# Sigmoid attention with a gated dense stage: the first group's keys cast and turned tile by tile, its values loaded as fp32 by SyncE

## The chip, the cores and the metric

The kernel runs on one core of a Trainium2 chip. The metric is the device time of one execution in microseconds (us); the time before is the median of 3 runs. Engines are named as in the profile: PE (TensorE, matmuls; PEld its weight loads), DVE (VectorE), ACT (ScalarE), POOL (GpSimd), SP (SyncE).

## The reference

```python
# q, k, v: (8, 12, 448, 64) fp32
scores = np.matmul(q, k.transpose(0, 1, 3, 2)) / np.sqrt(64) - np.log(448)
attn = 1.0 / (1.0 + np.exp(-scores))               # a sigmoid for each score, no sum over keys
x = np.matmul(attn, v)                             # (8, 12, 448, 64)
x = x.transpose(0, 2, 1, 3).reshape(8 * 448, 768)  # a token's 12 heads side by side
h = x @ w_in                                       # w_in (768, 2048)
g = h * (1.0 / (1.0 + np.exp(-beta * h)))
out = g @ w_out                                    # w_out (2048, 768), out (3584, 768) fp32
```

## The kernel before

Everything is computed in fp16 with fp32 sums. The 12 heads of a batch element are 3 groups of 4 heads (group g: batch element g // 3); a group's q and k are 128 rows of 32 positions times 4 heads, each row holding 14 blocks of 64 numbers. In such a row, position and head dimension are exchanged by a transpose of 32 x 32 squares on DVE (`transpose`, L196 for queries, L204 and L208 for keys), which reads pairs of fp16 as one 32-bit word. Keys are used in 3 tiles of 128 (`jt` 0 to 2) and a last one of 64 (`jt` 3); the word order of the raw row interleaves the three tiles (blocks i, j with i = 0..3 outside and tile j = 0..2 inside), and L204 sorts them while it turns them.

For a tile of keys, PE computes scores (`score`, L218) into a score tile of two PSUM banks, ACT takes the sigmoid of it into fp16 (`weigh`, L230), and `attend` (L291) multiplies by the values into a PSUM tile that DVE casts into `xT` (L300). `dense1` multiplies `xT` by `w_in` (L171), ACT and DVE apply the gate (L317, L320), and the result lies in `gt`; `dense2` and later steps multiply by `w_out`.

The order is written out by hand under `manual_schedule`, each engine working through its own list. The change lies in the first 20 us, where batch element 0 is begun with the first half of its queries (224 positions):

- SP loads group 0's q (first half) and k as fp32 into `staged`, a piece of `gt` that is still unused; then beta (L756). DVE and ACT cast them into the fp16 tile `raws[0]` (L747, L749, L750): of the keys, ACT the second half of the columns and DVE the first. DVE turns the queries and then all the keys.
- POOL loads the rest with DMAs that cast on the way (`load_one` L115, `load_v` L136 and L143, `load_w_in` L153), in the order q, k of groups 1 and 2, values of batch element 0 for all 12 heads (six DMAs: four for the 3 full tiles, two for the last 64 keys), the queries' second halves, and the 8 chunks of `w_in`, each for two of the 16 column blocks `dc` of `dense1`. At most eight POOL DMAs are under way: each waits for the landing of the eighth before it.
- `half_visit(g, c0, second)` computes the scores of group g for a half of the queries: key tiles 0 and 1 first, then with `second` tiles 2 and 3, with two score tiles each time. In this stage three score tiles exist (`share_psum(..., 3, 2)`), and two further banks, which `bank` gives out by turns for idle units and for `attend`.
- Idle units (`idle_units`, L740) are matmuls on zeros whose result nobody reads, 10 and a short one at the start, 4 (at the end 2) between half visits.
- `double_v_last` (L146) copies the values of the last 64 keys into the other 64 partitions; odd slots read them there.

The middle of it reads:

```python
        for g in range(QPB):
            for second in range(2):
                half_visit(g, 0, second)
                if 2 * g + second < 2 * QPB - 1:
                    idle_units(4 if g < QPB - 1 else 2)
        double_v_last(0)
        transpose(0, 0, NH, NB)
        attend(0, 0, QH)
        half_visit(0, QH, 0)
        attend(1, 0, QH)
```

After `attend(2, ...)` the PSUM banks are dealt out anew and `dense1` of the first 16 column blocks begins, mixed with the other half visits; then follows the long list of `STEPS`.

Of the kernel before, what the change touches and what calls it, by code (L numbers as in the profile page):

```python
# [8 lines left out]
FP32 = mybir.dt.float32  # L9
FP16 = mybir.dt.float16  # L10
# [3 lines left out]
def kernel(  # L14
# [10 lines left out]
    nc = tc.nc  # L25
# [3 lines left out]
    B, H, S, D = q.shape  # L29
    NTOK, DM = out.shape  # L30
    DFF = moe_w_in.shape[1]
    P = 128
    BLK = 32
    HQ = P // BLK
    NB = S // BLK
    PAIR = D // BLK
    JF = S // P
    KL = S - JF * P
    NF = JF * P // BLK
    NPAIR = H // 2  # L40
    QPB = H // HQ
# [5 lines left out]
    QH = S // 2  # L47
# [7 lines left out]
    vp = ctx.enter_context(tc.tile_pool(name="vp", bufs=2))  # L55
    qTp = ctx.enter_context(tc.tile_pool(name="qTp", bufs=3))
    kTp = ctx.enter_context(tc.tile_pool(name="kTp", bufs=3))
# [27 lines left out]
    def touch(i: int):  # L85
        used[i] = max(used.values()) + 1


    def bank(name: str, cols: int = S, hold=None):
        i = min((i for i in used if i not in held.values()), key=used.get)  # L90
        touch(i)
        if hold is not None:
            held[hold] = i
        pool = psum["one" if i < N_ONE else "late"]
        return pool.tile([P, cols], FP32, tag=f"one{i}", name=name)
# [12 lines left out]
    raws = {}  # L108
    vs = {}
# [19 lines left out]
    def last_base(s: int) -> int:  # L129
        return (s % 2 ^ swapped(s // 2)) * KL  # L130

    def load_v(b: int):
        vs[b] = vp.tile([P, H, JF + 1, D], FP16, tag="v16", name="v16")
        rows = v[b].rearrange("h (p c) d -> p h (c d)", c=NB)
        for i in range(HQ):
            nc.gpsimd.dma_start(  # L136
                out=vs[b][i * BLK : (i + 1) * BLK, :, 0:JF].rearrange("p h j d -> p h (j d)"),
                in_=rows[:, :, JF * i * D : JF * (i + 1) * D],
            )
        rows = v[b].rearrange("h (p c) d -> p h c d", c=NB)  # L140
        for c in range(NF, NB):
            lo = (c - NF) * BLK
            nc.gpsimd.dma_start(out=vs[b][lo : lo + BLK, :, JF], in_=rows[:, :, c])  # L143

    def double_v_last(b: int):
        nc.vector.tensor_copy(out=vs[b][KL:P, :, JF], in_=vs[b][0:KL, :, JF])  # L146

    WCH = 8
    WOUT = 2
# [30 lines left out]
    kT = {}  # L180
# [10 lines left out]
    def transpose(g: int, r: int, c0: int = 0, c1: int = NB):  # L191
        raw = raws[g][:, r]
        if r == 0:
            if g not in qT:
                qT[g] = qTp.tile([P, NB * BLK, PAIR], FP16, tag="qT", name="qT")
            nc.vector.transpose(  # L196
                out=in_order(g // QPB, qT[g][:, c0 * BLK : c1 * BLK]),
                in_=raw[:, c0:c1].rearrange("p c d -> p (c d)").bitcast(FP32),
            )
            return  # L200
        kT[g] = kTp.tile([P, S, PAIR], FP16, tag="kT", name="kT")
        to = kT[g].rearrange("p k e -> p (k e)").bitcast(FP32)
        frm = raw.rearrange("p c d -> p (c d)").bitcast(FP32).rearrange("p (c f) -> p c f", c=NB)
        nc.vector.transpose(  # L204
            out=to[:, 0 : JF * P].rearrange("p (j i q) -> p i j q", j=JF, i=HQ),
            in_=frm[:, 0:NF].rearrange("p (i j) f -> p i j f", j=JF),
        )
        nc.vector.transpose(  # L208
            out=to[:, JF * P :], in_=frm[:, NF:].rearrange("p c f -> p (c f)")
        )  # L210
# [45 lines left out]
    def half_visit(g: int, c0: int, second: int):  # L256
        slots = (2 * g, 2 * g + 1)
        scos = [score_tile() for _ in slots]
        plan = [(s, jt, sco, jt * QH) for jt in (0, 1) for s, sco in zip(slots, scos)]
        widths = [S, S]  # L260
        if second:
            plan = [(s, 2, sco, 0) for s, sco in zip(slots, scos)]
            plan += [(s, JF, scos[0], QH) for s in slots]
            widths = [S, QH]
        for i in range(0, len(plan), 2):
            for e in range(PAIR):
                for s, jt, sco, u0 in plan[i : i + 2]:
                    for hh in range(2):
                        score(sco, u0, s, jt, hh, e, c0, QH)
        homes = [None, None]  # L270
        if c0 == 0 and g < QPB - 1:
            home = outp.tile([P, 2 * S], FP32, tag="osb", name="early")
            home = home.bitcast(FP16).rearrange("p (x h s) -> p x h s", x=2, h=2)
            homes = [home[:, x] for x in range(2)]
        ats = {id(sco): weigh(sco, n, at) for sco, n, at in zip(scos, widths, homes)}
        for s, jt, sco, u0 in plan:
            at_tiles[s, jt, c0] = ats[id(sco)][:, :, u0 : u0 + QH]
# [435 lines left out]
    with tc.manual_schedule():  # L713
        raws[0] = rawp.tile([P, 2, NB, D], FP16, tag="raw", name="raw")
        wide = gt.rearrange("p a b -> p (a b)").bitcast(FP32)
        cut = NH * D
        early = [(0, 0, NH), (1, 0, NB)]
        staged = {}
        at = 0
        for r, c0, c1 in early:  # L720
            staged[r] = wide[:, at : at + (c1 - c0) * D]
            at += (c1 - c0) * D
            nc.sync.dma_start(  # L723
                out=staged[r],
                in_=(q, k)[r][0, 0:HQ].rearrange("h (p c) d -> (h p) (c d)", c=NB)[
                    :, c0 * D : c1 * D
                ],
            )
        nc.gpsimd.memset(dummy, 0.0)
        nc.scalar.activation(out=dummy, in_=dummy, func=AF.Sigmoid, bias=0.0, scale=1.0)  # L730

        still = gt[:, NDC - 1, 0:512]
        nc.vector.memset(still, 0.0)
        beta_in = sigp.tile([P, S], FP32, tag="sg", name="beta_in")[0:BLK, 0:P]
        nc.vector.memset(beta_in, 0.0)
        idle = bank("idle_ps", 512)

        def idle_units(n: int, cols: int = 512):
            for _ in range(n):
                nc.tensor.matmul(  # L740
                    idle[:, 0:cols], still[:, 0:P], still[:, 0:cols], start=True, stop=True
                )

        idle_units(10)
        idle_units(1, 256)
        raw = raws[0].rearrange("p r c d -> p r (c d)")
        nc.vector.tensor_copy(out=raw[:, 0, 0:cut], in_=staged[0])  # L747
        transpose(0, 0, 0, NH)
        nc.scalar.copy(out=raw[:, 1, cut:], in_=staged[1][:, cut:])  # L749
        nc.vector.tensor_copy(out=raw[:, 1, 0:cut], in_=staged[1][:, 0:cut])  # L750
        transpose(0, 1)
        for g in range(1, QPB):
            load_one(g, 0, 0, NH)
            load_one(g, 1)
        load_v(0)
        nc.sync.dma_start(out=beta_in[0:NDC], in_=moe_beta.rearrange("(c p) -> c p", p=P))  # L756
        for g in range(QPB - 1):
            load_one(g, 0, NH, NB)
        for c in range(WCH):
            if c == WCH // 2:  # L760
                load_one(QPB - 1, 0, NH, NB)
            load_w_in(c)
        for g in range(1, QPB):
            transpose(g, 0, 0, NH)
            transpose(g, 1)

        for g in range(QPB):
            for second in range(2):
                half_visit(g, 0, second)
                if 2 * g + second < 2 * QPB - 1:  # L770
                    idle_units(4 if g < QPB - 1 else 2)
        double_v_last(0)
        transpose(0, 0, NH, NB)
        attend(0, 0, QH)
        half_visit(0, QH, 0)
        attend(1, 0, QH)
        half_visit(0, QH, 1)
        for g in range(1, QPB - 1):
            transpose(g, 0, NH, NB)
        attend(2, 0, QH, (0,))  # L780
        attend(2, 0, QH, (1,))
        for i in range(P // BLK):
            part = slice(i * BLK, (i + 1) * BLK)
            nc.vector.transpose(out=beta_sb[part], in_=beta_in[:, part])
        load_qk(QPB)
        load_qk(QPB + 1)
        load_v(1)
        load_w_out(0, 0)
        load_w_out(1, 0)
        load_qk(QPB + 2)  # L790
        load_w_out(0, 1)
        load_w_out(1, 1)

        firsts.close()
        share_psum(ctx, seconds, 2, N_ONE, 2)
        first_half(4)
        half_visit(1, QH, 0)
        first_half(3)
        half_visit(1, QH, 1)
        transpose(2, 0, NH, NB)  # L800
        attend(0, QH, QH)
        first_half(1)
        half_visit(2, QH, 0)
        first_half(4)
        half_visit(2, QH, 1)
        attend(1, QH, QH)
        first_half(3)
        attend(2, QH, QH)
        first_half(1)
        follow(STEPS)  # L810
# [30 lines left out]
```

## Time and profile before

| | |
|---|---|
| time, median of 3 runs | 368.29 us (367.94 to 368.37) |
| the profiled execution | 368.51 us, of which the span of its instructions is 366.7 us |
| PE busy | 361.6 us, 99% |
| DVE, ACT, POOL busy | 271.7, 248.7, 154.3 us |
| granted TensorE clock in the profile's row | 1.0 throughout |
| DMA engines, first eight slices (73 us) | busy share 8 or 9 tenths |

Times in the profile count from the first instruction of the span. A row of the timeline has the start, the length, the engine, the line, what is written from what with the shapes, the number of instructions merged into it, and in brackets how long the engine had been idle and what released it. The chain of waits follows the work that ended last back to the start; a row of it is start, length, what. A DMA's row has the issuing engine, the count, the size, and the time from issue to landing.

### The profile page before, as it was taken

How to read it: one execution, taken by the hardware profiler on the slowest of the kernel's cores; microseconds unless marked ns; L12 is line 12 of the kernel's file. 1: busy time of each engine (PE TensorE's matmuls, PEld its weight loads, DVE VectorE, ACT ScalarE, POOL GpSimd, SP SyncE). 2: the span in 40 equal slices, each digit the busy share in tenths (PEclk: the TensorE clock that was granted, in tenths of full speed). 3: DMA queues.
4: the chain of work that ended last, by engine and by line, in shares of the span. 5: the costliest groups of instructions: out<-in, count | busy, mean ns of one | idle time of the engine just before them, and what ended most of it. 6: DMA issues, size and time to landing. Idle time of an engine off the chain costs nothing.

```text
span 366.7 us, 9126 instructions
## 1 busy us (share of the span) xinstructions
PE 361.6 (99%) x3677; PEld 238.0 (65%) x3677; DVE 271.7 (74%) x521; ACT 248.7 (68%) x409; POOL 154.3 (42%) x192
## 2 busy tenths in 40 slices
PE   8999999999999999999999999999999999999996
PEld 3478754457465685557857667666856687679763
DVE  3356569889995796876778678868878667678764
ACT  4987976789765797657865579977874859226410
POOL 7834523504413873117761445841630316316610
PEclk9999999999999999999999999999999999999999
DMA  8999999930363790416919363373303030030234
GB/s 168 184 197 201 199 206 198 236 39 2 50 139 52 160 152 2 74 64 111 156 13 149 52 137 52 49 81 89 52 1 89 2 88 2 0 88 0 56 68 138
DMA packets 42698, 34.76 MB, mean 95 GB/s; under 512 B 21904, under 2 KB 39200, under 8 KB 42656
## 3 DMA queue, kind: packets, MB, share of 16 engines
q0 software_dynamic: 36688, 22.47, 44.8%
q1 hardware_dynamic: 5968, 11.71, 11.5%
q8 instruction: 29, 0.48, 0.6%
q14 instruction: 13, 0.11, 0.1%
HBM read 45.62 MB, written 11.01 MB: 154 GB/s over the span
## 4 chain that ended last, share of the span: by engine, by line
PE 93%; DMA 3%; ACT 2%; DVE 1%; SPq 0%; issue 0%; ACTq 0%; DVEq 0%
PE m_ps L171 71%; PE sco L218 12%; PE av_ps L291 9%; DMA out_dram<-osb 2%; ACT attnT L230 1%; PE idle_ps L740 1%; DMA gt<-in_k_dram 1%; DVE osb L372 0%; SPq L602 0%; ACT osb L425 0%; DVE xT L300 0%; DVE kT L204 0%; ACT raw L749 0%; ACT osb L463 0%; SPq L723 0%
## 5 line engine op out<-in xcount | busy, mean ns | idle before, releaser
L230 ACT ACTIVATE attnT<-sco 128x896 f16<-128x896 f32 (+1 forms) x163 | 139.2, 908 | 37.8 <-PE sco L218 37.1
L372 DVE TENSOR_TENSOR osb<-m_ps,osb 128x448 f32<-128x448 f32 (+2 forms) x197 | 116.3, 596 | 51.1 <-PE m_ps L171 42.0
L171 PEld LDWEIGHTS <-w_in 128*128 128x128 f16 (+1 forms) x948 | 81.0, 100 | 18.8 <-issue 11.0
L171 PE MATMUL m_ps<-xT,w_in 128*128 128x224 f16 (+3 forms) x750 | 85.5, 266 | 0.3 <-ACT attnT L230 0.2
L492 POOL TENSOR_TENSOR gt<-osb,sg 128x448 f16<-128x448 f32 x26 | 29.5, 1135 | 117.8 <-ACT sg L425 107.7
L502 POOL TENSOR_TENSOR gt<-osb,sg 128x448 f16<-128x448 f32 x52 | 58.3, 1138 | 35.1 <-ACT sg L425 33.5
L425 ACT ACTIVATE sg<-osb,beta_sb 128x224 f32<-128x224 f32 (+1 forms) x104 | 54.0, 575 | 10.3 <-DVE osb L372 10.0
L171 PEld LDWEIGHTS <-sum 128*128 128x128 f16 (+1 forms) x444 | 39.9, 99 | 27.4 <-issue 3.6
L171 PEld LDWEIGHTS <-gt 128*128 128x128 f16 (+1 forms) x474 | 36.9, 102 | 25.7 <-issue 7.5
L171 PE MATMUL m_ps<-w_out,gt 128*128 128x384 f16 (+2 forms) x350 | 52.6, 324 | 0.0
L218 PE MATMUL sco<-qT,kT 32*128 32x448 f16 (+3 forms) x864 | 51.5, 340 | 0.3 <-ACT attnT L230 0.2
L171 PEld LDWEIGHTS <-w_S 128*128 128x128 f16 (+1 forms) x486 | 43.9, 99 | 7.0 <-issue 6.0
L171 PE MATMUL m_ps<-w_out,sum 128*128 128x384 f16 (+1 forms) x228 | 40.6, 327 | 0.0
L171 PE MATMUL m_ps<-w_T,sum 128*128 128x384 f16 (+1 forms) x216 | 40.3, 326 | 0.0
L300 DVE CAST xT<-av_ps 128x448 f16<-128x448 f32 (+1 forms) x54 | 28.4, 566 | 14.2 <-PE av_ps L291 14.1
L291 PE MATMUL av_ps<-attnT,v 128*64 128x448 f16 (+3 forms) x400 | 38.2, 343 | 0.0
L171 PE MATMUL m_ps<-xs,w_S 128*128 128x224 f16 (+1 forms) x330 | 36.2, 259 | 0.0
L291 PEld LDWEIGHTS <-v 128*64 128x64 f16 (+1 forms) x432 | 20.4, 108 | 17.7 <-issue 9.8
L425 ACT ACTIVATE osb<-m_ps,beta_sb 128x224 f32<-128x224 f32 x52 | 20.4, 448 | 15.4 <-PE m_ps L171 15.1
L218 PEld LDWEIGHTS <-kT 32*128 32x128 f16 (+1 forms) x864 | 13.5, 96 | 23.1 <-issue 21.5
L320 DVE TENSOR_TENSOR gt<-m_ps,sg 128x224 f16<-128x224 f32 (+1 forms) x40 | 16.6, 434 | 12.5 <-ACT sg L317 12.2
L463 ACT COPY osb<-m_ps 128x448 f32<-128x448 f32 x26 | 13.8, 535 | 17.7 <-PE m_ps L171 15.5
(50 smaller groups left out, 303.5 us busy)
## 6 DMA issues: line engine op xcount, KB each, us to landing
out_dram<-osb SPq DMA_DIRECT2D x100, 96.0 KB, 2.4
raw<-in_k_dram POOLq DMA_DIRECT2D x23, 224.0 KB, 5.7
raw<-in_q_dram POOLq DMA_DIRECT2D x21, 224.0 KB, 4.4
v<-in_v_dram POOLq DMA_DIRECT2D x32, 144.0 KB, 7.0
w_in<-in_moe_w_in_dram POOLq DMA_DIRECT2D x8, 384.0 KB, 10.3
w_out<-in_moe_w_out_dram POOLq DMA_DIRECT2D x4, 768.0 KB, 13.1
v<-in_v_dram POOLq DMA_DIRECT2D x16, 48.0 KB, 6.4
out_dram<-osb SPq DMA_DIRECT2D x4, 192.0 KB, 2.4
```

Source lines behind the costliest of these rows:

```text
L171: nc.tensor.matmul(to[c : c + step], hidden[:, c : c + step], weights, **({} if step == P else {"tile_position": (0, c)}), **flags,)
L218: nc.tensor.matmul(sco[base : base + nk, hh, u0 : u0 + n], kT[g][lo : lo + BLK, jt * P : jt * P + nk, e], qT[g][lo : lo + BLK, c0 : c0 + n ...
L230: nc.scalar.activation(out=at[:, :, 0:n], in_=sco[:, :, 0:n], func=AF.Sigmoid, bias=NEG_LOG_S, scale=MSCALE,)
L291: nc.tensor.matmul(av[hh * D : (hh + 1) * D, 0:n], vs[b][base : base + nk, 2 * (s % NPAIR) + hh, jt], at[base : base + nk, hh, 0:n], start ...
L300: nc.vector.tensor_copy(out=xTs[b][:, s % NPAIR, c0 : c0 + n], in_=av[:, 0:n])
L320: nc.vector.tensor_tensor(out=gt[:, dc, off : off + n], in0=m1[:, 0:n], in1=sg[:, 0:n], op=ALU.mult)
L372: nc.vector.tensor_tensor(out=out, in0=in0, in1=in1, op=op)
L425: nc.scalar.activation(out=out, in_=in_, func=AF.Sigmoid, bias=0.0, scale=beta_sb[:, dc : dc + 1])
L463: nc.scalar.copy(out=oa[:, 0], in_=m)
L492: nc.gpsimd.tensor_tensor(out=gt[:, 2 * d : 2 * d + 2, off : off + QH], in0=ob[:, 0], in1=sg, op=ALU.mult)
L502: nc.gpsimd.tensor_tensor(out=gt[:, dc, off : off + S].rearrange("p (h n) -> p h n", h=2), in0=oa[:, :, j], in1=sg, op=ALU.mult,)
L740: nc.tensor.matmul(idle[:, 0:cols], still[:, 0:P], still[:, 0:cols], start=True, stop=True)
```

## The change

Group 0's keys (0 to 3 of the 12 heads) are cast by tile: ACT casts tile 1 and then the last 64 keys, DVE tile 0 and later tile 2, and each tile is turned by a transpose of its own as soon as it is cast. The values of heads 0 to 3 are loaded by SP as fp32 into `firm`, a piece of `gt` that begins where the staged keys lie, and cast by three DVE copies into `vs[0]`, two of which write the last 64 keys' values to both halves of the partitions; POOL loads heads 4 to 11 alone, and `double_v_last` doubles those. `attend(0, 0, QH)` moves between the two last half visits of the first half, and idle units stand as (3, 4, 4, 4, none, 2) after the six half visits, 9 instead of 10 ahead of them. `idle_units` takes a PSUM bank at each call instead of one for all. Beta's DMA stands behind the values' on SP.

```diff
@@ -129,21 +129,24 @@
     def last_base(s: int) -> int:
         return (s % 2 ^ swapped(s // 2)) * KL
 
-    def load_v(b: int):
-        vs[b] = vp.tile([P, H, JF + 1, D], FP16, tag="v16", name="v16")
-        rows = v[b].rearrange("h (p c) d -> p h (c d)", c=NB)
+    def move_v(queue, to, b: int, h0: int, h1: int):
+        rows = v[b, h0:h1].rearrange("h (p c) d -> p h (c d)", c=NB)
         for i in range(HQ):
-            nc.gpsimd.dma_start(
-                out=vs[b][i * BLK : (i + 1) * BLK, :, 0:JF].rearrange("p h j d -> p h (j d)"),
+            queue.dma_start(
+                out=to[i * BLK : (i + 1) * BLK, h0:h1, 0:JF].rearrange("p h j d -> p h (j d)"),
                 in_=rows[:, :, JF * i * D : JF * (i + 1) * D],
             )
-        rows = v[b].rearrange("h (p c) d -> p h c d", c=NB)
+        rows = v[b, h0:h1].rearrange("h (p c) d -> p h c d", c=NB)
         for c in range(NF, NB):
             lo = (c - NF) * BLK
-            nc.gpsimd.dma_start(out=vs[b][lo : lo + BLK, :, JF], in_=rows[:, :, c])
-
-    def double_v_last(b: int):
-        nc.vector.tensor_copy(out=vs[b][KL:P, :, JF], in_=vs[b][0:KL, :, JF])
+            queue.dma_start(out=to[lo : lo + BLK, h0:h1, JF], in_=rows[:, :, c])
+
+    def load_v(b: int, h0: int = 0):
+        vs[b] = vp.tile([P, H, JF + 1, D], FP16, tag="v16", name="v16")
+        move_v(nc.gpsimd, vs[b], b, h0, H)
+
+    def double_v_last(b: int, h0: int = 0):
+        nc.vector.tensor_copy(out=vs[b][KL:P, h0:, JF], in_=vs[b][0:KL, h0:, JF])
 
     WCH = 8
     WOUT = 2
@@ -733,26 +736,54 @@
         nc.vector.memset(still, 0.0)
         beta_in = sigp.tile([P, S], FP32, tag="sg", name="beta_in")[0:BLK, 0:P]
         nc.vector.memset(beta_in, 0.0)
-        idle = bank("idle_ps", 512)
 
         def idle_units(n: int, cols: int = 512):
+            idle = bank("idle_ps", 512)
             for _ in range(n):
                 nc.tensor.matmul(
                     idle[:, 0:cols], still[:, 0:P], still[:, 0:cols], start=True, stop=True
                 )
 
-        idle_units(10)
+        idle_units(9)
         idle_units(1, 256)
         raw = raws[0].rearrange("p r c d -> p r (c d)")
         nc.vector.tensor_copy(out=raw[:, 0, 0:cut], in_=staged[0])
         transpose(0, 0, 0, NH)
-        nc.scalar.copy(out=raw[:, 1, cut:], in_=staged[1][:, cut:])
-        nc.vector.tensor_copy(out=raw[:, 1, 0:cut], in_=staged[1][:, 0:cut])
-        transpose(0, 1)
+        whole = [
+            t[:, 0 : NF * D].rearrange("p (i j d) -> p i j d", j=JF, d=D)
+            for t in (staged[1], raw[:, 1])
+        ]
+        kT[0] = kTp.tile([P, S, PAIR], FP16, tag="kT", name="kT")
+        words = kT[0].rearrange("p k e -> p (k e)").bitcast(FP32)
+
+        def key_cast(copy, j: int):
+            copy(out=whole[1][:, :, j], in_=whole[0][:, :, j])
+
+        def key_turn(j: int):
+            nc.vector.transpose(
+                out=words[:, j * P : (j + 1) * P].rearrange("p (i q) -> p i q", i=HQ),
+                in_=raws[0][:, 1, 0:NF]
+                .rearrange("p c d -> p (c d)")
+                .bitcast(FP32)
+                .rearrange("p (i j q) -> p i j q", i=HQ, j=JF)[:, :, j],
+            )
+
+        key_cast(nc.scalar.copy, 1)
+        nc.scalar.copy(out=raw[:, 1, NF * D :], in_=staged[1][:, NF * D :])
+        key_cast(nc.vector.tensor_copy, 0)
+        key_turn(0)
+        key_turn(1)
+        key_cast(nc.vector.tensor_copy, 2)
+        key_turn(2)
+        nc.vector.transpose(out=words[:, JF * P :], in_=raw[:, 1, NF * D :].bitcast(FP32))
+        firm = wide[:, cut : cut + HQ * (JF + 1) * D].rearrange(
+            "p (h j d) -> p h j d", h=HQ, d=D
+        )
+        move_v(nc.sync, firm, 0, 0, HQ)
         for g in range(1, QPB):
             load_one(g, 0, 0, NH)
             load_one(g, 1)
-        load_v(0)
+        load_v(0, HQ)
         nc.sync.dma_start(out=beta_in[0:NDC], in_=moe_beta.rearrange("(c p) -> c p", p=P))
         for g in range(QPB - 1):
             load_one(g, 0, NH, NB)
@@ -764,14 +795,17 @@
             transpose(g, 0, 0, NH)
             transpose(g, 1)
 
-        for g in range(QPB):
-            for second in range(2):
-                half_visit(g, 0, second)
-                if 2 * g + second < 2 * QPB - 1:
-                    idle_units(4 if g < QPB - 1 else 2)
-        double_v_last(0)
+        nc.vector.tensor_copy(out=vs[0][:, 0:HQ, 0:JF], in_=firm[:, :, 0:JF])
+        for lo in (0, KL):
+            nc.vector.tensor_copy(out=vs[0][lo : lo + KL, 0:HQ, JF], in_=firm[0:KL, :, JF])
+        for n in range(2 * QPB):
+            half_visit(n // 2, 0, n % 2)
+            if n == 2 * QPB - 2:
+                attend(0, 0, QH)
+                continue
+            idle_units((3, 4, 4, 4, 0, 2)[n])
         transpose(0, 0, NH, NB)
-        attend(0, 0, QH)
+        double_v_last(0, HQ)
         half_visit(0, QH, 0)
         attend(1, 0, QH)
         half_visit(0, QH, 1)
```

## The prediction

> **What bounds the kernel now.** I read the page first, then the chain of waits over the first 20 us (the change touches nothing later), the timeline of the first 45 us, and the DMA issues. One line of the page:
>
> ```profile
> PE 361.6 (99%) x3677; PEld 238.0 (65%) x3677; DVE 271.7 (74%) x521; ACT 248.7 (68%) x409; POOL 154.3 (42%) x192
> ```
>
> PE leaves 5 us of the span unfilled, and part of its busy time is idle units (L740), which compute nothing. They all lie before 14 us, so a gain has to come from there. The chain of waits, first 20 us (start, length, what):
>
> ```profile
> 1.18 3.56 DMA gt<-in_k_dram
> ...
> 4.76 0.57 ACT raw L749
> ...
> 5.36 0.59 DVE kT L204
> ...
> 6.00 0.62 PE sco L218 x16
> ...
> 16.29 3.08 ACT attnT L230 x4
> ...
> 19.42 0.64 PE m_ps L171 x5
> ```
>
> Group 0's keys land, are cast, are turned; only then does the first score start. The timeline shows who sets the pace afterwards, and where the values and weights stand:
>
> ```profile
> 1.19 4.66 PE L740 MATMUL idle_ps<-gt 128*128 128x512 f16 x11 [1.19 <-DVE gt L733]
> ...
> 4.76 0.39 DVE L750 CAST raw<-gt 128x448 f16<-128x448 f32 x1 [0.51 <-DMA gt<-in_k_dram]
> ...
> 5.36 0.58 DVE L204 STREAM_TRANSPOSE kT<-raw 128x384 f32<-128x384 f32 x1 [0.20 <-ACT raw L749]
> 5.86 0.20 DVE L208 STREAM_TRANSPOSE kT<-raw 128x64 f32<-128x64 f32 x1
> ...
> 6.55 1.04 PE L740 MATMUL idle_ps<-gt 128*128 128x512 f16 x4
> 6.66 6.28 ACT L230 ACTIVATE early<-sco 128x896 f16<-128x896 f32 x8 [1.33 <-PE sco L218]
> ...
> 13.08 6.29 ACT L230 ACTIVATE attnT<-sco 128x896 f16<-128x896 f32 x8
> ...
> 14.15 0.35 DVE L146 COPY v<-v 64x768 f16<-64x768 f16 x1 [4.27 <-DMA v<-in_v_dram]
> ```
>
> From its first sigmoid at 6.66 to 19.37 ACT stops only for gaps of 0.14 or 0.15: three score tiles circulate, a half visit needs two, and PE waits for ACT to empty one (14.00 ACT end, 14.05 next scores). At 19.42 the first dense matmul waits for the last sigmoid; from there PE runs without a wait on ACT or a DMA. So the end moves with ACT's first sigmoid, until something later becomes late. The candidate is this row of the DMA issues between 15.5 and 16.2 us, the sixth w_in chunk (KB, us to landing):
>
> ```profile
> w_in<-in_moe_w_in_dram POOLq DMA_DIRECT2D x1, 384.0 KB, 12.1
> ```
>
> Issued at 15.43, landed at 27.55, first used by PE at 28.14: 0.59 us to spare. The eighth (landed 31.50, used 32.09) has the same; the first w_out quarter (landed 43.62, used 44.30) 0.68.
>
> **The change, part by part.** *Keys.* Before, 1.24 us pass from the cast's start (4.76) to the first score (6.00). Now DVE casts tile 0 alone, 256 of 448 columns: 0.22 if in proportion to L750, 0.39 if a cast cost the same at any width; I take 0.26, near the proportion. ACT casts tile 1 beside it: 0.56 for 448 columns, and its sigmoids (0.54 for 448, 0.92 for 896) put about 0.16 of that as fixed, so 0.39, done at 5.15. Turning one tile is 128 columns; from 0.20 at 64 and 0.58 at 384, 0.28. A dependent DVE step followed after 0.03 (3.81 to 3.84), the score after 0.05. First score: 4.76 + 0.26 + 0.03 + 0.28 + 0.05 = 5.38. Tile 1's turn starts 0.08 before tile 0's ends, as L208 does behind L204: it ends at 5.53, in time for the second half of the first visit. That is 0.62 earlier. Tile 2 and the last 64 columns end near 6.15, and the second visit needs them past 7. The bound below: if the interleaved columns are taken as overlapping, DVE's cast waits for ACT's and the first score comes at 5.8, a gain of 0.1 to 0.2.
>
> *Clock of the first scores.* Eleven idle units took 4.66 us, 0.42 to 0.43 each, while four at 6.55 took 1.04 with their drain, 0.22 from start to start: PE works at half rate until about 6.1, although the page's clock row shows full rate throughout. The first 16 scores now fall before that. At full rate they take the 0.66 from PE's start to ACT's that is seen now (first sigmoid 6.04), at half rate 0.9 (6.30). So ACT starts 0.36 to 0.62 earlier in an execution like the profiled one. [...]
>
> *ACT's loop* stays: the same 16 sigmoids, the same three tiles. One idle unit fewer ahead of the second half visit changes nothing, since that visit's second tile waits for the first sigmoid (end 7.57, matmul 7.62). 12.70 us from first sigmoid to last, as now.
>
> *The first attend* moves ahead of the fifth visit's second half. PE has 13.06 to 14.05 there, 0.99, with two idle units in it; the attend takes 0.92 (chain: av_ps x16). Nothing on the path, if its values are there. The two idle units after that half take a PSUM bank from which DVE first casts (0.39 each); the scores behind them have until the next sigmoid ends, near 15.7. The cover is some 0.4.
>
> *Values.* SP's six DMAs write where the staged keys lay, so they wait for the last key cast, near 5.75. Six issues of 0.43 take SP to 8.3, with beta queued behind: it lands near 11 instead of 5.46 and is used at 19.55. DVE gets a cast of 768 columns (0.66 in proportion to L750) and two of 256 on 64 or fewer partitions (0.26 each): 1.2 us, in the 4.27 us in which it waits now; but they stand behind group 2's transposes, whose keys landed at 9.15 and will share engines with SP's transfer. The landing time is not in the trace: an SP store takes 2.4, the 448 KB of keys took 3.6, POOL's values 5.9 to 7.7 behind their queue. I take 3, near the SP rows: the last issue at 7.95 lands at 11, casts done by 12.2. The attend starts at 12.5 and its last tile, at its end, is read near 13.1. So it is hidden by 0.3 to 0.9. What DVE has next, group 0's remaining queries, needs a POOL transfer that landed at 14.26, with 0.6 to spare.
>
> *POOL.* Its six value DMAs carry 8 heads instead of 12, as many issues as before. The bytes read are the same, a third of them by another queue, and the DMA row is at 9 in all slices here, so I leave the w_in landings where they are. [...]
>
> *Sum.* ACT 0.36 to 0.62 earlier, 0.59 the most that the weights let through: I take 0.55. The profiled execution's 368.51 us (span 366.7 and 1.8 around it) becomes 367.95; the median of the runs is 0.22 below the profiled one, hence 367.7 for 368.29. A measurement of this kernel tells 0.2%, 0.74 us, from no change, so the forecast stands just inside.
>
> **Rivals.** *Half rate reaches further in other executions.* For: the turn at 6.1 is one execution's, and the runs of before spread over 0.43 us. If it comes at 7.5 to 8, before pays 0.25 in the first scores and 0.43 instead of 0.22 for each of four units, starting its second visit near 8.5; after, at 5.38 + 0.75 + 3 x 0.43 = 7.4. Gain 0.8 to 1.1, near 367.3, and lower if the weights land sooner. Against: it asks for a late turn in most executions.
>
> *Keys serial, or scores at half rate throughout*: gain 0.1 to 0.4, 368.0.
>
> *Values late: slower.* The attend stands in PE's order ahead of scores that ACT is waiting for; with a cover of 0.07 (0.99 less 0.92), each us by which its values are late is one on ACT. If SP's transfers land like POOL's values, 5.9 to 7.7 after issue, the last comes at 13.9 to 15.6, casts end 1.2 later, and PE stands 2 to 3.7 us past 13.1: 369.7 to 371.4. It decides from a landing at about 12: past 12.5 the 0.6 gained is gone, past 13.3 it is slower by over 0.74. For: DMA engines full, six issues in a row, one DVE queue. Against: SP's keys moved beside POOL's loads and took 3.6.
>
> *Weights late.* If SP's 448 KB as fp32 push POOL's queue back instead of replacing its share: the GB/s row shows up to 355 while SP's keys moved, so 1.2 to 1.3 us. Then the sixth chunk lands at 28.8 against a use at 27.6: PE waits 1.2 less what was gained, and the end is near 368.9. Against: POOL moves 229 KB of fp16 less, at 165 to 185 GB/s the same 1.3 us.
>
> **How the numbers follow.** Forecast 0.50, own range 367.3 to 368.1 (0.22 of it gains over 0.74, 0.28 not). Half rate further 0.18, faster. Keys serial or half rate 0.10, within. Values late 0.13: 0.11 slower, 0.02 within. Weights late 0.09: 0.07 slower, 0.02 within. Faster 0.22 + 0.18 = 0.40; within 0.28 + 0.10 + 0.04 = 0.42; slower 0.18. The range runs from 367.0, the large gain, to 368.9, the late weights; it leaves out the late values beyond that.
>
> **What would show it.** Right: the first score at 5.4, the first sigmoid between 6.0 and 6.3, the last one 12.7 later, first dense matmul near 18.8, no DMA as releaser on PE. Wrong: a first score at 5.8 (keys serial); DVE's wait for gt<-in_v_dram past 12, PE's first av_ps waiting on DVE (values late); PE m_ps <- DMA w_in (weights late); ACT gaps over 0.15 in the loop.

## The result and the profile after

The changed kernel takes 371.01 us (median of 6 runs, 369.91 to 372.31) against 368.32 for the kernel before in the same session: ratio 1.0073, 95% interval 1.0054 to 1.0093, so 0.7% slower. Its profiled execution takes 370.93 us with a span of 368.9; that of before took 368.51 with 366.7. The difference of 2.42 us is there at 22 us already: the first dense matmul starts at 21.85 instead of 19.42. The first 25 us of the chain of waits after (start, length, what):

```profile
1.19 3.24 DMA gt<-in_k_dram
...
4.45 0.44 DVE raw L760
...
4.98 0.52 DVE kT L763 x2
...
5.52 0.50 DVE raw L760
...
7.71 5.97 DMA gt<-in_v_dram
...
13.80 0.67 DVE v L798
...
14.52 1.66 PE av_ps L294 x14
16.18 1.01 PE sco L221 x15
...
18.73 3.08 ACT attnT L233 x4
...
21.85 2.46 PE m_ps L174 x24
```

The chain goes from the cast of the last key tile (5.52) to SP's issue of the values, then through a landing of 5.97 us, DVE's cast, and the attend that now stands ahead of the scores. The same stretch in the timeline:

```profile
5.35 0.57 PE L221 MATMUL sco<-qT,kT 32*128 32x224 f16 x16 [0.48 <-DVE kT L763]
...
5.96 6.28 ACT L233 ACTIVATE early<-sco 128x896 f16<-128x896 f32 x8 [0.91 <-PE sco L221]
...
6.09 2.05 SPq L135 DMA_DIRECT2D gt<-in_v_dram  x4
...
13.80 0.66 DVE L798 CAST v<-gt 128x768 f16<-128x768 f32 x1 [3.86 <-DMA gt<-in_v_dram]
...
14.52 1.66 PE L294 MATMUL av_ps<-early,v 128*64 128x224 f16 x16 [2.09 <-DVE v L798]
...
16.11 1.07 PE L221 MATMUL sco<-qT,kT 32*128 32x224 f16 x16
...
17.24 4.56 ACT L233 ACTIVATE attnT<-sco 128x896 f16<-128x896 f32 x6 [3.13 <-PE sco L221]
```

The keys' part worked, if less than forecast: the first score comes 0.90 us after the cast's start instead of 1.24, ACT's first sigmoid at 5.96 instead of 6.66 (0.32 of these 0.70 come from the keys landing at 4.42 instead of 4.74, which is this execution's luck). Then PE stands 2.09 us at the moved attend, and ACT waits 3.13 for the scores behind it. The difference between the two is in the granted clock of three stretches (columns: stretch and length, then busy time and instructions of each engine, clock, DMA share, GB/s):

```profile
11.00:14.41 3.41, 1.43 (x20) 0.60 (x18) 0.61 (x1) 2.96 (x4) 3.02 (x5) 1.00 1.39 213
14.41:17.83 3.42, 3.31 (x34) 1.49 (x34) 2.00 (x7) 0.59 (x1) 2.89 (x4) 0.50 1.46 196
17.83:21.85 4.02, 3.81 (x65) 2.16 (x65) 1.57 (x5) 3.83 (x6) 1.40 (x3) 1.00 1.45 198
```

After the stand PE gets half the clock for 3.42 us. In it fall the attend (1.66 us instead of the 0.92 in the chain before) and the next scores (1.07 instead of 0.69). The account, from first sigmoid to first dense matmul: 0.70 earlier at the start; 2.09 of standing, 0.74 in the attend, 0.38 in the scores, less 0.07 of cover, 3.14 later; together 2.44 against the 2.43 seen. Behind that no wait on PE is new.

Why the values land so late shows in the DMA view from 6.0 to 9.5 us, in which SP issues all six of their DMAs (queue: packets, MB, share; then issues with KB and us to landing):

```profile
q0 software_dynamic: 948, 0.61, 125.8%
...
gt<-in_v_dram SPq DMA_DIRECT2D x4, 96.0 KB, 5.9
...
gt<-in_v_dram SPq DMA_DIRECT2D x2, 32.0 KB, 6.2
```

In these 3.5 us there is not one packet of SP's queue (q1): all 948 belong to POOL's (q0), which had eight loads under way at SP's first issue. SP's packets begin after 9.5 (the trace has the first at 9.88, 3.8 us after the first issue), and the six landings come at 11.5 to 14.8. SP's first DMA of all, issued at 0.74 with no POOL load under way, had its first packet at 1.75; with that delay the values would have begun at 7.1. Yet POOL's queue was not simply first: between 10 and 12 us SP's queue moved 0.38 MB and POOL's 0.12, although four POOL loads issued before SP's landed only at 10.45 to 13.25. How the DMA engines choose is not shown here.

### The profile page after: what moved, and what is told of

It reads as the page before. It is cut to its first block, busy times and chain, and to the rows that moved or that the text cites. A ratio compares the mean times of both kernels' runs of the same rounds, so it can differ in the third digit from the quotient of the medians.

```text
span 368.9 us, 9147 instructions
## 1 busy us (share of the span) xinstructions
PE 361.5 (98%) x3675; PEld 238.0 (65%) x3675; DVE 273.6 (74%) x527; ACT 248.8 (67%) x410; POOL 153.9 (42%) x192
## 4 chain that ended last, share of the span: by engine, by line
PE 94%; DMA 2%; ACT 1%; DVE 1%; SPq 1%; issue 0%; DVEq 0%
PE m_ps L174 73%; PE sco L221 11%; PE av_ps L294 9%; DMA gt<-in_v_dram 2%; DMA gt<-in_k_dram 1%; ACT attnT L233 1%; SPq L135 0%; DVE raw L760 0%; PE idle_ps L743 0%; DVE v L798 0%; DVE kT L763 0%; SPq L726 0%; DVE osb L375 0%; DVEq L798 0%; DVEq L763 0%
```

## The experiments

The theory was: **values late**. The whole loss hangs on when the cast of SP's values is done, and that is late because POOL's loads, issued earlier, are served first. Rivals were that the attend's new place costs by itself, that SP's short rows are slow at any time, that the added traffic slows the rest, and that the keys' part costs something. Each ratio is to the kernel before on the same chip.

**Keys alone** (e1_keys_only). The kernel before, with this edit and 9 idle units at the start:

```diff
-        nc.scalar.copy(out=raw[:, 1, cut:], in_=staged[1][:, cut:])
-        nc.vector.tensor_copy(out=raw[:, 1, 0:cut], in_=staged[1][:, 0:cut])
-        transpose(0, 1)
+        key_cast(nc.scalar.copy, 1)
+        nc.scalar.copy(out=raw[:, 1, NF * D :], in_=staged[1][:, NF * D :])
+        key_cast(nc.vector.tensor_copy, 0)
+        key_turn(0)
...
```

> The kernel before with the tile-by-tile casts and turns of the keys alone (and 9 idle units at the start); values as before. Theory 'values late' (all of the loss is PE's wait for the cast of the values that SP loads): the first score comes at 5.4 and the first sigmoid near 6.0 as in the changed kernel, the loop behind it is as long as ever, and the end is 0.4 to 0.6 us earlier than before, near 367.8. Rival 'nothing gets through' (the weights' landings hold the dense stage back): the first sigmoid is earlier, but PE waits for w_in, and the time is that of before, 368.3 within 0.2.

Measured 368.48 against 368.67, ratio 0.9994 (0.998 to 1.0008): no difference that could be told. The first dense matmul starts at 18.90, 0.52 earlier than in the profile of before, so neither theory as written holds: the gain reaches the dense stage and does not show in the time. The profiled execution (369.36, one of the slower of this kernel) shows a place where some of it may go, in the chain of waits between 150 and 183 us:

```profile
151.59 7.16 DMA out_dram<-osb
...
158.87 0.57 DVE osb L567
...
159.48 2.76 PE m_ps L171 x16
```

A store that SP issued at 151.59, with two of POOL's loads under way, landed after 7.16 us; the output tile that it frees was waited for by DVE and then for 0.48 us by PE. In the kernel before, SP's stores of this moment took up to 6.14 us beside two POOL loads, and PE had no wait there; whether the changed keys have a part in this wait is asked further below.

**Values alone** (e2_values_only). The changed kernel with the key casts and the turn of before, the reverse of the edit above.

> The changed kernel with the keys cast and turned as before (two casts, one turn), so the values' part alone. 'The end is set by when the values land': the last key cast ends at 5.3 to 5.4 instead of 6.0, SP issues 0.7 earlier and the values land 0.5 to 0.7 earlier, so this is faster than the changed kernel although its first score comes 0.3 to 0.6 later: near 370.0, ratio to before about 1.004. 'The two parts add up': without the keys' gain it is 0.5 slower than the changed kernel, ratio about 1.009.

Ratio 1.0024 (1.0007 to 1.004), less than half the loss of the whole change, and less than either theory expected. SP issues at 5.20 instead of 6.09 and the last values land at 13.96 instead of 14.78. PE stands for a third of the time:

```profile
13.62 1.38 PE L294 MATMUL av_ps<-early,v 128*64 128x224 f16 x16 [0.69 <-DVE v L774]
```

and the granted clock stays full behind it: the scores that follow take 0.70, not 1.07. So the two parts do not add up: the last of the tile-by-tile casts ends at 6.01 where the last cast here ends at 5.17, and that delays the values. The two first dense matmuls lie 1.56 us apart (21.85 and 20.29): 0.90 of it is the attend's later start, the rest the half rate behind it.

**Fast keys, values as early as there** (e9_tail_place). The changed kernel with another landing place:

```diff
-        firm = wide[:, cut : cut + HQ * (JF + 1) * D].rearrange(
+        room = cut + NF * D
+        firm = wide[:, room : room + HQ * (JF + 1) * D].rearrange(
...
```

> The changed kernel with the values' landing place moved so that it overlaps only the last 128 columns of the staged keys (cast by ACT near 5.0); SP then issues near 5.1 instead of 6.1, the fast keys stay. 'The end is set by when the values land': issue and landing are those of the run with the values' part alone (10.8 to 14.0), so the time is that of that run although the first score comes 0.5 earlier: ratio to before 1.001 to 1.004, about 1.2 us faster than the changed kernel. 'The keys' part costs something of its own': it stays near 1.007.

Ratio 1.0028 (1.0007 to 1.005), that of the values alone. SP issues from 5.17, the landings come at 11.03 to 14.11, PE stands 0.97 and 0.28 at the attend. With about the same landing, keys that are quicker make no difference that these runs could tell: the end is set by the values.

**Values from 1.65 us on** (e3_own_place). The same edit with a place that nothing uses (`room = cut + NB * D`).

> The changed kernel with the values' landing place moved to columns of gt that nothing uses yet, so SP issues them from 1.6 us on instead of 6.1. 'Values late by their issue': they land by 9, PE does not wait at the moved attend, no half rate follows, and the time is 367.7 to 368.3 (it may give up to 0.6 back if group 1's keys, which then share the engines, land 1.2 us later). Rival 'the attend's place costs by itself' (its 0.92 us stands ahead of scores that ACT needs): with the values at hand it is still slower than before by about 0.9, near 369.2. Rival 'the values' transfer is slow whenever it is issued' (5 to 6 us to landing): landing at 7 to 10, in time all the same, 368.

Ratio 1.0037 (1.0023 to 1.0052), slower than any of the three theories had it (370.16). PE doesn't wait for the values, but everything else comes later: group 0's keys at 5.24, the first score at 6.07, group 1's keys at 8.68, the fourth `w_in` chunk at 24.81 instead of the 22.57 of the kernel before. A line from its waits over the first 30 us, and one from its DMA issues:

```profile
PE m_ps L174 <- DMA w_in<-in_moe_w_in_dram: 0.7, 1, 0.7
```

```profile
v<-in_v_dram POOLq DMA_DIRECT2D x1, 96.0 KB, 8.5
```

(the second, from the issues between 1.7 and 4 us, is a POOL load that took 6.3 in the changed kernel). SP's six took 5.9 to 8.1 us to land, though at the first of them POOL had issued a single load and at the last only seven: beside each other the two queues moved 0.12 to 0.18 MB/us in all between 5 and 7 us, as counted at the destination in steps of half a us, no more than POOL's queue alone in the kernel before (0.12 to 0.18). The traffic alone costs about half of what the whole change did.

**The clock** (e4_idle_cover). The changed kernel with one line:

```diff
             if n == 2 * QPB - 2:
+                idle_units(10)
                 attend(0, 0, QH)
```

> The changed kernel with 10 idle units between the fifth half visit and the moved attend, about 2.2 us of work in the 2.1 us in which PE waited. If the half rate after the wait (attend 1.66 instead of 0.92, next scores 1.07 instead of 0.69) comes from PE standing still, the second part of the loss goes: 0.4 to 0.7 us faster than the changed kernel, near 370.4, and the runs spread less. If the whole loss is the wait itself, 371.0 stays.

Ratio 1.0047 (1.0031 to 1.0063) instead of 1.0073, 370.38, as expected for a loss that is in part the clock's. With work on zeros in place of standing the clock stayed full:

```profile
12.37 2.33 PE L743 MATMUL idle_ps<-gt 128*128 128x512 f16 x10
14.63 1.06 PE L294 MATMUL av_ps<-early,v 128*64 128x224 f16 x16
15.62 0.70 PE L221 MATMUL sco<-qT,kT 32*128 32x224 f16 x16
```

The attend and the scores behind it take 1.06 and 0.70 us, where the changed kernel has 1.66 and 1.07, and the first dense matmul starts at 20.99 instead of 21.85. In the runs of the changed kernel itself the fastest (369.91) is the one with a mean granted clock of 1.000, the slowest (372.31) the one with 0.989; the other four have 0.994 or 0.995, which is about what one such half rate takes from the mean (half of 3.42 us is 0.46% of the span of 368.9). Here all six runs have 0.998 or more and lie within 0.87 us instead of 2.40. (The two ratios' intervals overlap a little, so the clocks say more than the times.) In the changed kernel's profile the half rate begins at 14.41, at the end of the 2.09 us of standing; of the 3.41 us before it PE was busy for 1.43. In e7 below it stood for 1.53 and was busy for 2.08 of a stretch of the same length, from 14.74 on; the clock stayed full there, with 0.58 for the 16 scores behind the stand. Whether the length of the stand alone decides is not shown.

**The attend back in its old place** (e5_attend_back). The changed kernel with `attend(0, 0, QH)` behind the last half visit.

> The changed kernel with the first attend back behind the last half visit. 'Values late': the values are cast at 14.5 and 15.6 as in the changed kernel, PE reaches the attend near 14.0 and is held to about 15.9, where the scores behind it could have begun at 15.1: about 0.8 lost, 0.6 to 0.7 gained by the keys, near 368.4. Rival 'the traffic of SP's values slows the rest' (loads, weights): it stays slower by over 1.5, near 370.

Ratio 1.0024 (1.0000 to 1.0048), 369.59, between the two times expected: most of the loss goes with the attend's place, since there PE needs the values 1.6 us later. What is left has two waits in a row:

```profile
15.38 0.28 PE L294 MATMUL av_ps<-early,v 64*64 64x224 f16 x2 [0.35 <-DVE v L800]
16.47 0.58 PE L221 MATMUL sco<-qT,kT 32*128 32x224 f16 x16 [0.81 <-DVE qT L199]
```

The second was in no theory: DVE's casts of the late attend stand ahead of the turn of group 0's remaining queries.

**Both mended** (e10_tail_back). The values' place of e9, the attend back, and `transpose(0, 0, NH, NB)` ahead of it.

> The same with the first attend back behind the last half visit, and group 0's remaining queries turned ahead of it on DVE. 'Values late' only where PE asks for them before they are there: PE reaches the attend near 14.0, the casts end near 14.0 and 14.8, the scores behind it begin near 15.1 as the loop wants them, and the keys' 0.5 gets through: 0.3 to 0.5 us faster than before. If the added traffic (weights up to 0.5 later) holds the dense stage, PE waits for w_in after 27 and the time is that of before.

The first dense matmul starts at 19.01 in the profile, where the kernel before has 19.42, PE's wait for the queries is down to 0.16, and one wait of 0.13 for `w_in` follows. Still the ratio is 1.0014 (1.0002 to 1.0025): slightly slower than before, where faster or the same had been expected. The profiled execution, 368.27, is its fastest run, so what holds the others can't be read from it.

**POOL held back** (e6_pool_held). One tiny POOL copy ahead of POOL's six value DMAs, reading a piece of the last cast key tile:

```diff
+        nc.gpsimd.tensor_copy(out=dummy, in_=raw[:, 1, 2 * D : 2 * D + 1])
         load_v(0, HQ)
```

> The changed kernel with one tiny POOL copy ahead of POOL's six value DMAs that reads a piece of the last cast key tile, so that POOL issues them from about 6.3 instead of 3.5, after SP's first. 'DMAs are served about in the order in which they are issued, whichever engine issued them': SP's six find only the keys and queries of groups 1 and 2 ahead of them (landed at 9.2), so they land from about 9.5 to 12.5 instead of 11.5 to 14.8, PE's wait at the moved attend shrinks from 2.1 to under 0.5, and the time falls to 368.5 to 369.5. 'SP's short rows are slow whenever they run': they land 5.4 to 6.2 after issue again, 371.

POOL now issues these from 7.09. From the DMA view between 6.6 and 9.3 us:

```profile
q0 software_dynamic: 375, 0.38, 86.2%
q1 hardware_dynamic: 286, 0.20, 26.7%
...
gt<-in_v_dram SPq DMA_DIRECT2D x4, 96.0 KB, 3.9
...
gt<-in_v_dram SPq DMA_DIRECT2D x2, 32.0 KB, 4.6
```

SP's packets run in this stretch beside POOL's (the first at 7.71, 1.2 us after SP's first issue, with three POOL loads under way instead of eight), its six DMAs take 3.5 to 4.8 us instead of 5.4 to 6.25, and the first lands at 9.99, right behind group 2's keys at 9.55. So the delay comes from what POOL had issued before, not from SP's rows. PE stands 0.58 at the attend instead of 2.09. The time expected was wrong all the same: 371.23, ratio 1.0067 (1.005 to 1.0083), since POOL's own first four value loads now land 1.7 to 2.6 us later than in the changed kernel and the `w_in` chunks 2.2 to 2.6, and PE waits for `w_in` at 25.55 (0.63) and for 0.25 to 0.51 in three places behind. The keys landed late too, at 5.13, in this profile, which is of the slowest of the six runs (372.19).

**Group 0's values by POOL, ahead of the others** (e7_pool_first). SP's values and DVE's casts are gone; `move_v(nc.gpsimd, vs[0], 0, 0, HQ)` stands ahead of the same for heads 4 to 11, and one DVE copy doubles the last 64 keys' values.

> The changed kernel without SP's values and DVE's casts of them: POOL loads heads 0 to 3 in six DMAs (cast on the way) ahead of the six for heads 4 to 11; tile-by-tile keys and the attend's new place are kept. 'Values late': heads 0 to 3 land by 11, PE does not wait at the moved attend (reached near 12.4), no half rate, first dense matmul near 18.9, 368.0 to 368.4; 'the attend's place costs by itself': first dense matmul 0.9 later, near 19.8, 369.2. Six more POOL issues of 0.6 may hold the weights back; then PE waits for w_in after 24.

The values are there at 10.46, and ACT's loop runs unbroken over the moved attend:

```profile
5.92 6.28 ACT L233 ACTIVATE early<-sco 128x896 f16<-128x896 f32 x8 [0.81 <-PE sco L221]
12.34 3.07 ACT L233 ACTIVATE attnT<-sco 128x896 f16<-128x896 f32 x4
16.69 3.07 ACT L233 ACTIVATE attnT<-sco 128x896 f16<-128x896 f32 x4 [1.27 <-PE sco L221]
```

From the first sigmoid to the end of the twelfth 9.49 us, as before (6.66 to 16.15): the attend's place costs nothing by itself. But the time is 372.73, ratio 1.0105 (1.0088 to 1.0122), far from what was expected, and the waits of PE say why:

```profile
PE m_ps L174 <- DMA w_in<-in_moe_w_in_dram: 2.8, 4, 1.2
PE sco L221 <- DVE qT L199: 1.5, 1, 1.5
```

With six more DMAs in POOL's queue, which has at most eight under way in the traces of before and after, the queries behind them land at 15.58 instead of 14.26 and each weight chunk about 4 us late. The expectation had named this as a maybe and given it no price.

**Where the keys' gain goes** (e8_keys_8idle, then the kernel before and the keys alone, each profiled twice more). The first has 8 idle units at the start.

> Keys tile by tile alone, as in the run with the keys' part, with 8 idle units instead of 9 at the start, since there the first score stood behind the last idle unit (5.43). First score at 5.35, first dense matmul near 18.8, 0.6 earlier than before. If that gets through to the end: 0.5 us faster than before. If, as in that run, something far behind gives most of it back (PE waits of 0.5 and 0.6 near 160 and 180 us, for an output tile whose store lands late): within 0.3 of before.

Ratio 0.9998 (0.9988 to 1.0008), the second of the two cases. Its profile has the first dense matmul at 19.14 and again PE waiting near 160 us, 0.57 for the same output tile. The four further profiles:

> The kernel before, profiled once more. 'A late store holds PE near 160 us only when PE runs ahead': no wait of PE over 0.2 us between 150 and 190 us, span 366.6 to 366.9. 'Such waits come and go by execution, whatever the kernel': a wait of 0.3 to 1 us there in this or the next look.

> The kernel with the keys' part alone, profiled once more. 'A late store holds PE only when PE runs ahead': first dense matmul near 18.9, and again a wait of 0.3 to 0.7 near 159.5, so the span is that of before. 'By execution': no such wait, span 0.3 to 0.5 under that of before.

> The kernel before, third profile: as in the first of these looks.

> The keys' part alone, third profile: as in the second of these looks.

None of the four has a wait near 160 us, and the spans are 366.8 and 366.6 for before, 366.5 and 366.1 for the keys alone, as 'by execution' had it. Other waits come and go too: before showed 0.38 for `w_out` at 44.8 us in one of these profiles and none in the other; keys alone 0.30 for `w_in` at 28.1 in one and none in the other. The first dense matmul starts at 19.42, 19.32 and 19.16 in three profiles of before, at 18.90, 18.89 and 19.14 with the keys by tile, so the gain at the front is some 0.3 us on average. The single times of these four are 368.53 and 368.50 for before, 368.37 and 368.10 for the keys alone. What arrives of it at the end is below what 12 runs can tell; the wait near 160 us was seen in one profile each of e1, e8, e3 and e6 and in none of the others, the three of before among them, but that it takes the gain is not shown. No version was clearly faster than the kernel before, and none had the values in time without delaying other loads; that the stand and its half rate make the loss rests on the account of the first 22 us and on e4 and e5.

## Why the prediction was wrong

*Step that failed: the landing of the values.* The sum took 3 us from issue to landing, "near the SP rows", last landing at 11. It measured 5.4 to 6.25 and 14.78. The rows chosen were of SP with little or nothing of POOL's beside it: the keys were issued at 1.18 ahead of POOL's first load, and between 3 and 4 us, while they moved, the trace has 113 packets of SP's queue and 14 of POOL's, so that "SP's keys moved beside POOL's loads" misreads it; the page's 2.4 is a median over stores of which most had no load beside them. The trace of before held the right row; its DMA issues between 121 and 124 us, where POOL was issuing five loads:

```profile
out_dram<-osb SPq DMA_DIRECT2D x7, 96.0 KB, 5.2
```

From the trace's issues and landings: the 58 stores of before that found no POOL load under way landed after 1.9 us (median), the 17 that found four or more after 4.9, but so did, after 4.7, the 18 that found two. At 6.1 us eight POOL loads were under way. The prediction named full engines as the reason for the rival and then took a row from another state of the queue.

*The rival that came true* was "values late", with a chance of 0.13 and 369.7 to 371.4 for landings of 5.9 to 7.7: 371.01 lies in it. Its rule, slower by over 0.74 from a landing at 13.3, gives 370.5 for the 14.78 seen; the last 0.5 is about what e4 took away (0.63), the half rate after the stand, which no part of the prediction priced (it charged one us of ACT for one us of PE). The range ended at 368.9 because this case's far end was left out.

*First score.* Mis-sized: 0.62 earlier forecast, 0.34 measured from the cast's start. The cast of 256 columns took 0.42 and the later one 0.49, not 0.26; the turn began 0.11 behind the cast instead of 0.03, and the score 0.37 behind the turn's start instead of 0.33. With that the last key cast ended at 6.01 instead of 5.75 and SP's issue came at 6.09. In e6 both casts took 0.29, as did the later one in e1, near the estimate.

*Clock of the first scores.* PE's turn to full rate was taken at 6.1 from one execution. It came at 4.2 in the changed kernel's profile (from there an idle unit took 0.22 us, not 0.43), so the first scores ran at full rate here, 16 in 0.57 us; in e8 they took 0.90 from 5.43 on.

*ACT's loop, the attend's place, the idle units' cover*: right, shown by e7. *DVE's added casts*: 0.66 measured as forecast, and 0.69 instead of 0.52 for the two small ones together, within the room if the values had been there. *Weights*: forecast unchanged; seven of the eight chunks landed 0.2 to 0.5 later and one 0.2 earlier, about what a second profile of the kernel before differs by (0.3 to 0.5 later). They are a term where the values come early (e3: 1.4 to 2.3 later, a wait of 0.7).

*From the first dense matmul to the end.* The sum passed the front's gain through in full. e1 and e8 could not find it at the end; this step was taken from one execution without waits, and others have them.

## What to carry to other kernels

Before a load is moved to another engine's queue, look in the trace for DMAs that this engine issued while the other queue was full, and take the landing from those; the same row from an empty moment was off by a factor of two (3 us taken, 5.4 to 6.25 measured). Here the attend that waited in PE's own order cost its wait of 2.09 us and half the clock for the 3.42 us behind it; values that may be late belong where something else can run first. Two parts of a change can work against each other through a shared buffer: here the tile-by-tile casts freed the landing place later (6.01 instead of 5.17).

## What the runs showed of the hardware

- With eight POOL loads under way at SP's first issue, SP's queue had no packet for 3.8 us (6.09 to 9.88), and its six DMAs landed 5.4 to 6.25 us after issue; with five of the eight issued later (e6) the first packet came after 1.2 us and the six landed after 3.5 to 4.8.
- PE standing for 2.09 us was followed by half the clock for 3.42 us in the profiled execution, and five of the six runs have a mean clock of 0.989 to 0.995; with stands of 0.69 (e2), of 0.97 and 0.28 (e9) and of 1.53 (e7) the clock stayed full behind them in the profiled executions: the next 16 scores took 0.70, 0.70 and 0.58, against 1.07 after the 2.09.
- The same DVE cast of 128 x 256 from fp32 to fp16 took 0.29 to 0.52 us in different executions. In e6, where POOL issued nothing during them, both took 0.29, but so did the second one in e1 (at 5.59), in the middle of four POOL issues (3.55 to 6.12); the cause stays open.
